# Attention backward on one core: the key-side score gradients are taken from DMA transposes, and the sums for dk, dv and dq are kept in SBUF

## The chip, the core and the metric

The kernel runs on one NeuronCore of a Trainium2 chip. TensorE (PE) multiplies matrices from SBUF into PSUM, VectorE (DVE) and ScalarE (ACT) work element by element and empty PSUM, GpSimd (POOL) does some element work from SBUF, and SyncE (SP) issues the transfers. Each engine takes its instructions in order and waits on semaphores for the others. The metric is the device time of one execution in microseconds.

## What is computed

The program returns the output of a gated mix of multi-head attention and a state-space convolution, and the gradients of twelve of its inputs, for a sequence of 2048 tokens and a width of 576. The change touches the attention alone: 32 heads of width 18.

```python
def _A_ref(x, wqkv, wo):
    B, S, D = x.shape
    H = 32
    Dh = D // H
    qkv = (lambda x, *d: x.transpose(*d))((x @ wqkv).reshape(B, S, 3, H, Dh), 2, 0, 3, 1, 4)
    q, k, v = qkv[0], qkv[1], qkv[2]
    scores = jnp.einsum("bhqd,bhkd->bhqk", q, k) * (Dh ** -0.5)
    p = _softmax(scores, axis=-1)
    o = jnp.einsum("bhqk,bhkd->bhqd", p, v)
    return (lambda x, *d: x.transpose(*d))(o, 0, 2, 1, 3).reshape(B, S, D) @ wo
...
_out, _vjp = jax.vjp(_f, A_x, A_wqkv, A_wo, B_A_re, B_A_im, B_B_re, B_B_im, B_C_re, B_C_im, B_log_dt, B_Dskip, gate_w)
_grads = _vjp(grad_out)
```

With P the softmax and dP = dO V^T, the backward pass needs dS = P (dP - delta), where delta is the sum of dO times O over a head; then dq = dS K (summed over keys), dk = dS^T Q and dv = P^T dO (both summed over queries).

## The kernel before

Four stages follow each other: the projections, which leave q, k, v and dO in DRAM in two layouts; attention, forward and backward; the products with the output projection, which read the attention output O; and the state-space part.

Attention works on eight groups of four heads (NG = 8, j = 0 to 3 within a group). Each head fills a strip of 32 partitions, and heads on different strips can share a pass of PE. The 2048 tokens are cut into four blocks of 512 (NQ = 4, KB = 512) and sixteen tiles of 128 (NT = 16, index i). There are four kinds of score tile, each 128x512, and 2048 of each kind over the program:

- P1: keys on partitions, queries along the row. `qk` multiplies K and Q, ACT takes the exponential and leaves the tile PT. It feeds the forward sum over keys, accA.
- P2: the same layout. `qk` multiplies V with dOaT (dO over the softmax sum, with -delta in an extra column), DVE multiplies by PT and leaves ds. It feeds the sum for dq, accB.
- P3S: queries on partitions, keys along the row. The score is computed again, and ACT takes the exponential again (eb). It feeds the sum for dv, accA.
- P3D: the same layout. dP is computed again and DVE multiplies by eb. It feeds the sum for dk, accB.

Every score tile has one matmul of 19 rows by 128 columns over 512 columns (written as `19*128 19x512`), one instruction of ACT or DVE, and one accumulating matmul (`pv`), whose output is 32 partitions by 512. The sums run in PSUM over all sixteen tiles; the last tile of a block calls `finish`, which copies the sum out. At the end of a P1 block, `post_forward` turns the sum to token layout (ps_o), divides by the softmax sum (O_tok, in SBUF), forms dOa and delta on POOL and DVE, and turns dOa back (dOaT). `post_grad` turns dq, dk and dv of a whole group and stores them in dqkv_d.

The order is written by hand. The list `blocks` pairs a P1 block with a P2 block, or a P3S block with a P3D block. A step issues two score matmuls for ACT and two for DVE, on the other pair of heads, then the accumulating matmuls of two steps before (LAG = 2), then ACT's and DVE's instructions. `run_piece` issues one piece of `post_forward` or `post_grad` in every third step. PE, ACT, DVE and POOL run in this order; SP's transfers are placed by the scheduler. PSUM gives three slots each to tags S (P1, P3S and all the transposes) and dP (P2, P3D), one to accA and one to accB. All tiles of a group that are loaded (`load_group`) have two buffers.

The state-space part has 36 DMA transposes of its own (L930), of E1e tiles of 128x4096 in 2-byte elements.

Of the kernel before, what the change touches and what calls it, by code (L numbers as in the profile page):

```python
# [20 lines left out]
def build(tc, aps, dbg_aps=None, stages=("s1", "attn", "post", "s4", "final")):  # L21
# [39 lines left out]
    with ExitStack() as gctx:  # L61
# [15 lines left out]
        mid1_cm = tc.tile_pool(name="mid1", bufs=1)  # L77
        mid1 = mid1_cm.__enter__()
        O_tok = mid1.tile([P, NT, D], BF, name="O_tok")
# [6 lines left out]
        Vtok_d = dram.tile([P, NT * H * HP], BF, name="Vtok_d")  # L86
        dO_d = dram.tile([P, NT, D], BF, name="dO_d")
# [168 lines left out]
        if "attn" in stages:  # L256
# [4 lines left out]
            with ExitStack() as ctx:  # L261
                ctx.enter_context(tc.manual_schedule(engines={mybir.EngineType.PE, mybir.EngineType.Activation, mybir.EngineType.DVE, mybir.EngineType.Pool}))
                ga = ctx.enter_context(tc.tile_pool(name="ga", bufs=2))
                ptp = ctx.enter_context(tc.tile_pool(name="ptp", bufs=18))
                work = ctx.enter_context(tc.tile_pool(name="awork", bufs=2))
                apsp = ctx.enter_context(tc.tile_pool(name="aps", bufs=1, space=bass.MemoryType.PSUM))
                ident_f = const.tile([P, P], F32, name="ident_f")
# [5 lines left out]
                grp_t = {}  # L273
                dOa2 = []
                for u in range(2):
                    dOa_u = work.tile([P, NT, 4, HP], BF, tag=f"dOa{u}", bufs=1, name=f"dOa{u}")
                    nc.gpsimd.memset(dOa_u, 0.0)
                    dOa2.append(dOa_u)

                def load_group(g):  # L280
                    T = {}
                    for nm, src in (("QaT", QaT_d[g]), ("KaT", KaT_d[g]), ("VaT", VaT_d[g])):
                        T[nm] = ga.tile([P, S], BF, tag=nm, name=nm + "_g")
                        nc.sync.dma_start(T[nm], src)
                    for nm, src in (("Qtok", Qtok_v), ("Ktok", Ktok_v), ("Vtok", Vtok_v)):
                        T[nm] = ga.tile([P, NT, 4, HP], BF, tag=nm, name=nm + "_g")
                        nc.sync.dma_start(T[nm], src[:, :, 4 * g:4 * g + 4, :])
                    T["dO"] = ga.tile([P, NT, 4, DH], BF, tag="dO", name="dO_g")
                    nc.sync.dma_start(T["dO"].rearrange("p t a b -> p t (a b)"), dO_d[:, :, 4 * g * DH:4 * (g + 1) * DH])
                    T["dOa"] = dOa2[g % 2]  # L290
                    T["dOaT"] = ga.tile([P, S], BF, tag="dOaT", name="dOaT_g")
                    for nm in ("dqT", "dkT", "dvT"):
                        T[nm] = ga.tile([P, S], BF, tag=nm, bufs=1, name=nm + "_g")
                    T["PT"] = {}
                    grp_t[g] = T

                def ps1(tag, name, dt=F32, w=KB):
                    return apsp.tile([P, w], dt, tag=tag, bufs=3, name=name)

                later = []  # L300

                def pieces(fs):
                    later.append(list(fs))

                def run_piece():
                    if later:
                        later[0].pop(0)()
                        if not later[0]:
                            later.pop(0)

                def post_forward(g, b, acc):
                    T = grp_t[g]
                    t0 = b * TPQ
                    c0 = g * 4 * DH
                    h0 = 4 * g
# [6 lines left out]
                    def f1():  # L322
                        st["po"] = apsp.tile([P, TPQ, 4, HP], F32, tag="S", bufs=3, name="ps_o")
                        for qi in range(TPQ):
                            nc.tensor.transpose(st["po"][:, qi, :, :].rearrange("p a b -> p (a b)"), st["oT"][:, qi * P:(qi + 1) * P], ident_f)
                        rl = work.tile([P, TPQ, 4], F32, tag="rl", name="rl")
                        nc.vector.reciprocal(rl, st["po"][:, :, :, DH])  # L327
                        rlb = rl.unsqueeze(3).to_broadcast([P, TPQ, 4, DH])
                        Ov = O_tok[:, t0:t0 + TPQ, c0:c0 + 4 * DH].rearrange("p t (a b) -> p t a b", b=DH)
                        dOv = T["dO"][:, t0:t0 + TPQ, :, :]  # L330
                        da = T["dOa"][:, t0:t0 + TPQ, :, :]
                        nc.vector.tensor_tensor(Ov, st["po"][:, :, :, 0:DH], rlb, op=A.mult)
                        nc.gpsimd.tensor_tensor(da[:, :, :, 0:DH], dOv, rlb, op=A.mult)  # L333
                        prod = work.tile([P, TPQ, 4, DH], F32, tag="prod", name="prod")
                        nc.gpsimd.tensor_tensor(prod, da[:, :, :, 0:DH], Ov, op=A.mult)
                        dl = work.tile([P, TPQ, 4], F32, tag="dl", name="dl")
                        nc.vector.tensor_reduce(dl, prod, axis=AX.X, op=A.add)
                        nc.gpsimd.tensor_scalar(da[:, :, :, DH], dl, -1.0, None, op0=A.mult)

                    def f2():  # L340
                        pt = apsp.tile([P, KB], BF, tag="S", bufs=3, name="ps_doT")
                        for qi in range(TPQ):
                            nc.tensor.transpose(pt[:, qi * P:(qi + 1) * P],
                                                T["dOa"][:, t0 + qi, :, :].rearrange("p a b -> p (a b)"), ident_bf)
                        nc.scalar.copy(T["dOaT"][:, b * KB:(b + 1) * KB], pt)

                    return [f0, f1, lambda: None, f2]

                def post_grad(g, nm, which):
                    T = grp_t[g]  # L350
                    c0 = which * D + g * 4 * DH
                    HT = NT // 2

                    def half(u):
                        def f():
                            pt = apsp.tile([P, HT, 4, HP], BF, tag="S", bufs=3, name="ps_dt")
                            for t in range(HT):
                                tt_ = u * HT + t
                                nc.tensor.transpose(pt[:, t, :, :].rearrange("p a b -> p (a b)"), T[nm][:, tt_ * P:(tt_ + 1) * P], ident_bf)
                            dtk = work.tile([P, HT, 4, DH], BF, tag="dtk", name="dtk")  # L360
                            nc.scalar.copy(dtk, pt[:, :, :, 0:DH])
                            nc.sync.dma_start(dqkv_d[:, u * HT:(u + 1) * HT, c0:c0 + 4 * DH], dtk.rearrange("p t a b -> p t (a b)"))
                        return f
                    return [half(0), half(1)]

                def qk(kind, g, b, i, j):
                    T = grp_t[g]
                    r0 = HP * j
                    if kind == "P1":
                        l, r = T["KaT"], T["QaT"]  # L370
                    elif kind == "P2":
                        l, r = T["VaT"], T["dOaT"]
                    elif kind == "P3S":
                        l, r = T["QaT"], T["KaT"]
                    else:
                        l, r = T["dOaT"], T["VaT"]
                    tg = "S" if kind in ("P1", "P3S") else "dP"
                    ps = ps1(tg, "ps_" + kind)
                    mm(ps, lhsT=l[r0:r0 + DA, i * P:(i + 1) * P], rhs=r[r0:r0 + DA, b * KB:(b + 1) * KB], tile_position=(r0, 0))
                    return ps  # L380

                e3 = {}

                def elem(kind, g, b, i, j, ps):
# [70 lines left out]
                for n in range(len(act_s) + LAG):  # L455
                    cur = []
                    if n < len(act_s):
                        for (blk_, i, jj) in (act_s[n], dve_s[n]):
                            if blk_ is None:
                                continue  # L460
# [765 lines left out]
```

## Time and profile before

| | |
|---|---|
| time, median of 3 runs | 5774.57 us (5774.31 to 5775.28) |
| profiled execution | 5779.55 us, span 5777.8 us |
| PE busy over the span | 3879.6 us, 67%, 34473 matmuls |
| DVE busy over the span | 4022.2 us, 70% |
| ACT busy over the span | 3207.5 us, 56% |
| POOL busy over the span | 607.7 us, 11% |
| DVE, ACT, PE busy from 1200 to 1600 us | 362.45, 321.77, 382.92 of 400 us |
| DMA share there | 0.05 |

A row of the costliest groups reads: line, engine, operation, output<-inputs, shapes and count; then busy time, mean time of one in ns, and the idle time of the engine just before such instructions, with what ended it. In a timeline a row gives the start, the length and, at its end, how many instructions ran back to back. The engine called SPq in it is SP's queue, and its rows are issues of transfers. A matmul's end is modelled, and matmuls on different strips overlap, so the distance from one start to the next says more of PE than its busy time.

### The profile page before, as it was taken

The page shows a single profiled execution, that of the slowest core. Times are in us where ns is not written, and L with a number is a line of the kernel's source. Part 1 is how long each engine was busy: PE and PEld are TensorE (multiplying, and loading weights), DVE is VectorE, ACT ScalarE, POOL GpSimd, SP SyncE. Part 2 cuts the span into 40 slices and gives each one's busy share as a digit, 9 for nine tenths or more (in the row PEclk, how much of TensorE's full clock was granted, in tenths as well). Part 3 has the DMA queues.
Part 4 walks back from the last instruction along what each step waited for, and adds up shares of the span by engine and source line. Part 5 has one row for each costly group of instructions (what it writes and reads, how often), then busy time and mean ns, then how long its engine had stood idle before and what let it go on. Part 6 is the DMA issues. An engine that isn't in the chain of part 4 may idle for free. (4 is left out here: it accounts for less than half of the span.)

```text
span 5777.8 us, 90570 instructions
## 1 busy us (share of the span) xinstructions
PE 3879.6 (67%) x34473; PEld 1452.2 (25%) x34473; DVE 4022.2 (70%) x7458; ACT 3207.5 (56%) x6150; POOL 607.7 (11%) x845
## 2 busy tenths in 40 slices
PE   6687999999999999999999987832222222222221
PEld 4462111212212122121221237711111222222210
DVE  4334899898998989989899973330017667776668
ACT  3336788787887778878788562310004444444421
POOL 1000000000000000000000000030002333333330
PEclk9999999999999999999999558855555555555555
DMA  2122000101001010010000013032235444444436
GB/s 96 59 74 65 11 2 7 25 1 29 3 7 25 1 29 3 7 25 1 20 3 1 7 38 118 32 102 65 66 92 124 113 113 113 115 115 115 111 92 168
DMA packets 599927, 316.83 MB, mean 55 GB/s; under 512 B 523198, under 2 KB 571520, under 8 KB 589634
## 3 DMA queue, kind: packets, MB, share of 16 engines
q1 hardware_dynamic: 599490, 311.05, 20.8%
q8 instruction: 269, 4.41, 0.3%
q14 instruction: 168, 1.38, 0.1%
HBM read 203.53 MB, written 69.71 MB: 47 GB/s over the span
## 5 line engine op out<-in xcount | busy, mean ns | idle before, releaser
L398 DVE TENSOR_TENSOR ds<-ps_P3D,eb 128x512 bf16<-128x512 f32 x2048 | 1293.5, 686 | 128.0 <-PE ps_P3D L30 83.9
L398 DVE TENSOR_TENSOR ds<-ps_P,PT 128x512 bf16<-128x512 f32 x2048 | 1288.8, 686 | 100.6 <-PE ps_P L30 96.7
L394 ACT ACTIVATE eb<-ps_P3S 128x512 bf16<-128x512 f32 x2048 | 1109.0, 595 | 258.8 <-PE ps_P3D L30 181.7
L390 ACT ACTIVATE PT<-ps_P 128x512 bf16<-128x512 f32 x2048 | 1107.5, 596 | 213.0 <-PE ps_P L30 131.7
L30 PE MATMUL ps_P3D<-VaT_g,dOaT_g 19*128 19x512 bf16 x2048 | 791.4, 593 | 16.6 <-DVE ds L398 16.0
L30 PE MATMUL ps_P<-dOaT_g,VaT_g 19*128 19x512 bf16 x2048 | 757.1, 591 | 0.5 <-DVE ds L398 0.4
L30 PE MATMUL ps_P<-QaT_g,KaT_g 19*128 19x512 bf16 x2048 | 675.1, 597 | 72.1 <-DMA KaT_g<-KaT_d 37.8
L30 PE MATMUL ps_P3S<-KaT_g,QaT_g 19*128 19x512 bf16 x2048 | 671.2, 597 | 30.9 <-ACT eb L394 28.4
L30 PE MATMUL accA<-PT,Vtok_g 128*32 128x512 bf16 x2048 | 625.4, 608 | 6.6 <-DMA Vtok_g<-Vtok_d 6.5
L30 PE MATMUL accA<-eb,dOa 128*32 128x512 bf16 x2048 | 626.3, 608 | 0.0
L30 PE MATMUL accB<-ds,Qtok_g 128*32 128x512 bf16 x2048 | 625.8, 608 | 0.0
L30 PE MATMUL accB<-ds,Ktok_g 128*32 128x512 bf16 x2048 | 625.0, 607 | 0.0
L30 PE MATMUL uvr<-RX,E1e 128*128 128x64 bf16 x576 | 72.4, 291 | 647.9 <-DVE E1e L891 647.9
L30 PEld LDWEIGHTS <-E1e 128*128 128x128 bf16 x1152 | 119.8, 124 | 724.3 <-DVE E1e L891 629.4
L333 POOL TENSOR_TENSOR dOa<-dO_g,rl 128x288 bf16<-128x288 bf16 x32 | 21.5, 673 | 2663.7 <-DVE rl L327 2663.7
L824 DVE TENSOR_SCALAR xs<-xs,msk 128x3072 bf16<-128x3072 bf16 x21 | 21.4, 1020 | 375.9 <-DMA xs<-in_A_x_dram 375.9
L30 PEld LDWEIGHTS <-dOa 128*32 128x32 bf16 x2048 | 107.4, 101 | 634.6 <-issue 634.6
L837 ACT COPY mst<-psM 128x512 f32<-128x512 f32 x36 | 22.1, 613 | 438.4 <-PE psM L30 362.2
L30 PEld LDWEIGHTS <-Vtok_g 128*32 128x32 bf16 x2048 | 106.6, 101 | 585.1 <-issue 577.7
L30 PE MATMUL psM<-xs,gyp 128*32 128x128 bf16 x576 | 54.7, 550 | 259.8 <-DMA xs<-in_A_x_dram 133.6
L30 PEld LDWEIGHTS <-KaT_g 19*128 19x128 bf16 x2048 | 104.9, 99 | 480.6 <-issue 452.0
L30 PE MATMUL ybp<-Rw,E1n 128*128 128x31 bf16 x1152 | 71.4, 233 | 224.9 <-POOL Rw L972 219.5
(332 smaller groups left out, 5561.0 us busy)
## 6 DMA issues: line engine op xcount, KB each, us to landing
abuf<-ath_d SPq DMA_DIRECT2D x36, 1024.0 KB
thb<-ath_d SPq DMA_DIRECT2D x36, 1024.0 KB
T0w<-Kp_d SPq DMA_DIRECT2D x36, 512.0 KB
dqkv_d<-dtk SPq DMA_DIRECT2D x48, 144.0 KB
dqkv_tok<-dqkv_d SPq DMA_DIRECT2D x1, 6912.0 KB
Md_d<-mst SPq DMA_DIRECT2D x144, 36.0 KB
x_tok<-in_A_x_dram SPq DMA_DIRECT2D x2, 2304.0 KB
ga_d<-ga_st SPq DMA_DIRECT2D x16, 288.0 KB
```

Source lines behind the costliest of these rows:

```text
L30: return nc.tensor.matmul(out, lhsT=lhsT, rhs=rhs, start=start, stop=stop, **kw)
L333: nc.gpsimd.tensor_tensor(da[:, :, :, 0:DH], dOv, rlb, op=A.mult)
L390: nc.scalar.activation(out, ps, ACT.Exp)
L394: nc.scalar.activation(out, ps, ACT.Exp)
L398: nc.vector.tensor_tensor(out, ps, e, op=A.mult)
L824: nc.vector.tensor_scalar(xs[:, dl, :, :], xs[:, dl, :, :], msk[:, dl:dl + 1], None, op0=A.mult)
L837: nc.scalar.copy(mst[:, :, 0:P], psM)
```

## The change

P3D goes. P1, P2 and P3 (the former P3S) are issued together in one loop over G, a step of which has two of each. A "unit" is a group and a query block (32 units of 32 steps). P2 and P3 of a unit run OFF = 37 steps behind its P1.

- When the four heads of a key tile i have their ds, SP issues one DMA transpose of the 128x2048 tile. It leaves dsT, queries on partitions, which feeds the sum for dk. There are four buffers of ds and three of dsT (two key tiles each).
- The sums for dv, dq and dk no longer run in PSUM over sixteen tiles. Bursts of eight matmuls (`dv_burst`, `dq_burst`), or two halves of eight narrower ones (`dk_half`), fill one PSUM slot (accB), and DVE adds it to a sum in SBUF in f32. Sums of dv and dk run on over the four query blocks of a group.
- `post_forward` has its POOL instructions on DVE now, and stores O to DRAM (O_d) per unit; the stage after attention loads it as O_tok. `store_grad` turns f32 sums of 512 tokens, with one copy of 128x288 on ACT each.
- PSUM: four slots S, two dP, one accO, one accB. VaT, Ktok and Qtok of a group have one buffer, QaT, KaT and Vtok two.

```diff
-        O_tok = mid1.tile([P, NT, D], BF, name="O_tok")
+        O_d = dram.tile([P, NT, D], BF, name="O_d")
...
+                    for nm, src, nb in (("QaT", QaT_d[g], 2), ("KaT", KaT_d[g], 2), ("VaT", VaT_d[g], 1)):
+                        T[nm] = ga.tile([P, S], BF, tag=nm, bufs=nb, name=nm + "_g")
...
-                        nc.gpsimd.tensor_tensor(da[:, :, :, 0:DH], dOv, rlb, op=A.mult)
-                        nc.gpsimd.tensor_tensor(prod, da[:, :, :, 0:DH], Ov, op=A.mult)
+                        nc.vector.tensor_tensor(da[:, :, :, 0:DH], U["dO"], rlb, op=A.mult)
+                        nc.vector.tensor_tensor(prod, da[:, :, :, 0:DH], Ob, op=A.mult)
...
+                def dv_burst(g, b, kq, half):
+                    acc = accB("accV")
+                    for n_ in range(2):
+                        ii = 2 * half + n_
+                        for j in range(4):
+                            mm(acc[HP * j:HP * (j + 1), :], lhsT=U["dOa"][:, ii, j, :], rhs=U["eb"].pop((kq, ii, j)),
+                               start=(n_ == 0), stop=(n_ == 1), tile_position=(0, HP * j))
+                    def ev():
...
+                            nc.vector.tensor_tensor(a_, a_, acc, op=A.add)
...
+                def dk_half(g, b, p, h, st):
+                    for qb in (2 * h, 2 * h + 1):
+                        for j in range(4):
+                            mm(acc[HP * j:HP * (j + 1), 0:2 * P].rearrange("p (a b) -> p a b", b=P), lhsT=grp_t[g]["Qtok"][:, b * TPQ + qb, j, :],
+                               rhs=U["dsT", p][:, :, j * TPQ + qb, :], start=(qb == 0), stop=(qb == 3), tile_position=(0, HP * j))
...
+                        if s == 4 and b == NQ - 2 and g + 1 < NG:
+                            load_group(g + 1)
...
+                            par_ = (s2 + OFF) % 2
+                            jo = 2 * (1 - par_) + x
+                            rows.append(("P3", g, b, (kq, ii), jo, row("P3", g, b, T["QaT"][:, qt * P:(qt + 1) * P], T["KaT"][:, kq * KB:(kq + 1) * KB], jo)))
+                            j2 = 2 * par_ + (1 - x)
+                            rows.append(("P2", g, b, i2, j2, row("P2", g, b, T["VaT"][:, i2 * P:(i2 + 1) * P], U["dOaT"], j2)))
+                    if G % 4 == 1 and G2 >= 4:
+                            evs.append(dv_burst(g, b, q_ // 2, q_ % 2))
+                    if G % 4 == 2 and G2 >= 5:
+                            evs.append(dq_burst(g, b, q_))
+                    if G % 4 in (3, 0) and G2 >= 10:
+                            e_ = dk_half(g, b, q_, h_, dkst)
...
+                            if U["dsn", i] == 4:
+                                nc.sync.dma_start_transpose(out=U["dsT", p][:, i % 2, :, :], in_=U["ds"][i].rearrange("p j q -> p (j q)"))
...
+                nc.sync.dma_start(O_tok, O_d)
```

The order of the built programs shows it at three places. The first is PE in the middle of attention. Before, a step of a P3S and a P3D block is four score matmuls and the accumulating matmuls of an earlier step (numbers tell buffers apart; each matmul has its weight load ahead of it):

```order
L30 LDWEIGHTS QaT_g_7148
L30 MATMUL ps_P3S_11556<-KaT_g_7150,QaT_g_7148 128x512
L30 LDWEIGHTS QaT_g_7148
L30 MATMUL ps_P3S_11558<-KaT_g_7150,QaT_g_7148 128x512
L30 LDWEIGHTS dOaT_g_7162
L30 MATMUL ps_P3D_11560<-VaT_g_7152,dOaT_g_7162 128x512
L30 LDWEIGHTS dOaT_g_7162
L30 MATMUL ps_P3D_11562<-VaT_g_7152,dOaT_g_7162 128x512
L30 LDWEIGHTS dOa0_7144
L30 MATMUL accA_11241<-eb_11528,dOa0_7144 32x512
```

Now, on PE, a step has six score matmuls, and then a burst; this one is the first half of a dk burst, from dsT:

```order
L30 MATMUL ps_P1_11242<-QaT_g_8512,KaT_g_8514 128x512
L30 LDWEIGHTS QaT_g_7147
L30 MATMUL ps_P3_11244<-KaT_g_7149,QaT_g_7147 128x512
L30 LDWEIGHTS VaT_g_7151
L30 MATMUL ps_P2_11246<-dOaT_10725,VaT_g_7151 128x512
L30 LDWEIGHTS KaT_g_8514
L30 MATMUL ps_P1_11248<-QaT_g_8512,KaT_g_8514 128x512
L30 LDWEIGHTS QaT_g_7147
L30 MATMUL ps_P3_11250<-KaT_g_7149,QaT_g_7147 128x512
L30 LDWEIGHTS VaT_g_7151
L30 MATMUL ps_P2_11252<-dOaT_10725,VaT_g_7151 128x512
L30 LDWEIGHTS Qtok_g_7157
```

P3D and its weights dOaT are gone, P1 stands beside P2 and P3 of a later place in the loop (here of another group, as the buffer numbers of QaT and KaT show), and the accumulating matmuls come as bursts.

The second place is DVE in the middle of a unit, now:

```order
L519 TENSOR_TENSOR ds_28045<-ps_P2_28025,PT_26776 128x512
L519 TENSOR_TENSOR ds_28045<-ps_P2_28031,PT_26776 128x512
L379 TENSOR_TENSOR dvacc_25831<-dvacc_25831,accV_28033 128x512
L519 TENSOR_TENSOR ds_28045<-ps_P2_28056,PT_26776 128x512
L519 TENSOR_TENSOR ds_28045<-ps_P2_28062,PT_26776 128x512
L396 TENSOR_TENSOR dqa_27817<-dqa_27817,accQ_28064 128x512
L519 TENSOR_TENSOR ds_28113<-ps_P2_28089,PT_26839 128x512
L519 TENSOR_TENSOR ds_28113<-ps_P2_28095,PT_26839 128x512
L519 TENSOR_TENSOR ds_28113<-ps_P2_28123,PT_26839 128x512
L519 TENSOR_TENSOR ds_28113<-ps_P2_28129,PT_26839 128x512
L420 TENSOR_TENSOR dkacc_25799<-dkacc_25799,accK_28097 128x256
```

In four steps DVE has eight products and three additions; before, it had sixteen products in the same work (eight P2, eight P3D) and no addition.

The third place is SP where one group gives way to the next (the first rows are stores and loads of the old group, VaT is the next group's and QaT that of the group after it):

```order
L525 DMA_TRANSPOSE dsT_11662<-ds_11693 128x16x128 [waits DMAHW6_49,DVE_49]
L323 DMA O_d_79<-Ob_11784 128x4x72 [waits DMAHW7_49,DVE_49]
L294 DMA dO_b_12837<-dO_d_80 128x4x72 [waits DMAHW0_49,DVE_49]
L525 DMA_TRANSPOSE dsT_11823<-ds_11770 128x16x128 [waits DMAHW1_49,DVE_49]
L282 DMA QaT_g_13000<-QaT_d_73 128x2048 [waits DMAHW2_49,PE_49]
L282 DMA VaT_g_8516<-VaT_d_75 128x2048 [waits DMAHW3_49,PE_49]
L525 DMA_TRANSPOSE dsT_11823<-ds_11855 128x16x128 [waits DMAHW4_49,DVE_49]
L282 DMA KaT_g_13002<-KaT_d_74 128x2048 [waits DMAHW5_49]
L341 DMA dqkv_d_81<-dtk_11939 128x4x72 [waits DMAHW6_49,Activation_49]
L285 DMA Ktok_g_8520<-Ktok_d_77 128x16x128 [waits DMAHW7_49,PE_49]
```

The transposes are a new kind of row between the loads, and VaT and Ktok wait for PE here; before, the next group's VaT had a buffer of its own and stood far ahead of its use. The DMAHW marks are eight completion counters that are used in turn, so a transfer waits for ones eight or so places back.

More of the change, by code (lines that the diff above doesn't have):

```diff
@@ L345, in f2 @@
[L345 to L350, printed above, removed]
-                    c0 = which * D + g * 4 * DH
[L352 to L364, printed above, removed]
@@ L367, in qk, with row @@
+                def row(kind, g, b, l, r, j):
                     T = grp_t[g]
                     r0 = HP * j
[L369 to L377, printed above, removed]
@@ L427, in build @@
[L427 to L430 removed]
+                    tg, nb = ("dP", 2) if kind == "P2" else ("S", 4)
+                    ps = apsp.tile([P, KB], F32, tag=tg, bufs=nb, name="ps_" + kind)
+                    mm(ps, lhsT=l[r0:r0 + DA], rhs=r[r0:r0 + DA], tile_position=(r0, 0))
+                    return ps
+                NST = 2 * NT
+                NU = NG * NQ
```

319 lines of the change are left out of this document (174 added, 145 removed).

## The prediction

> **What bounds the kernel now.** First the page: the span, against 5779.55 us for the profiled execution (5774.57 is the median of the runs shown), and its costliest groups.
>
> ```profile
> span 5777.8 us, 90570 instructions
> L398 DVE TENSOR_TENSOR ds<-ps_P3D,eb 128x512 bf16<-128x512 f32 x2048 | 1293.5, 686 | 128.0 <-PE ps_P3D L30 83.9
> L398 DVE TENSOR_TENSOR ds<-ps_P,PT 128x512 bf16<-128x512 f32 x2048 | 1288.8, 686 | 100.6 <-PE ps_P L30 96.7
> L394 ACT ACTIVATE eb<-ps_P3S 128x512 bf16<-128x512 f32 x2048 | 1109.0, 595 | 258.8 <-PE ps_P3D L30 181.7
> L390 ACT ACTIVATE PT<-ps_P 128x512 bf16<-128x512 f32 x2048 | 1107.5, 596 | 213.0 <-PE ps_P L30 131.7
> ```
>
> Instructions of one engine overlap at their ends, so the pitch is busy time by count: 1293.5/2048 = 0.632 us for a DVE product, 1109.0/2048 = 0.541 us for an exp on ACT. The timeline shows where the stage begins and ends, and a piece from its middle.
>
> ```profile
> 463.75 0.61 PE L30 MATMUL ps_P<-QaT_g,KaT_g 19*128 19x512 bf16 x3 [12.21 <-DMA KaT_g<-KaT_d]
> ...
> 1299.41 7.00 DVE L398 TENSOR_TENSOR ds<-ps_P,PT 128x512 bf16<-128x512 f32 x11
> ...
> 1300.62 2.32 ACT L390 ACTIVATE PT<-ps_P 128x512 bf16<-128x512 f32 x4 [0.20 <-PE ps_P L30]
> ...
> 1301.95 0.61 PE L30 MATMUL accA<-PT,Vtok_g 128*32 128x512 bf16 x2
> ...
> 1302.50 0.61 PE L30 MATMUL ps_P<-QaT_g,KaT_g 19*128 19x512 bf16 x2
> ...
> 1303.18 0.61 PE L30 MATMUL accA<-PT,Vtok_g 128*32 128x512 bf16 x2
> ...
> 3412.74 1.06 PE L359 MATMUL ps_dt<-ident_bf,dkT_g 128*128 128x128 bf16 x8
> ```
>
> Attention takes 3413.80 - 463.75 = 2950 us, half of the kernel. DVE runs eleven products without a gap in 7.00 us; a step of two takes 1.25 us, the same as PE from one accA to the next (1301.95 to 1303.18). ACT rests 0.20 in 2.5. So DVE ends last; ACT is next at 2 x 0.541 = 1.08 a step.
>
> PE is the third. At the end of the stage nothing holds it, and its own pace shows:
>
> ```profile
> 3408.59 1.03 PE L30 MATMUL accB<-ds,Qtok_g 128*32 128x512 bf16 x4
> ...
> 3408.99 0.64 PE L30 MATMUL accA<-eb,dOa 128*32 128x512 bf16 x2
> ...
> 3409.55 1.03 PE L359 MATMUL ps_dt<-ident_bf,dvT_g 128*128 128x128 bf16 x8
> ```
>
> Four accumulating matmuls on different 32-column strips run together; a second round on the same strips starts 0.40 later, and a matmul of another kind 0.56 after that. Above, the kinds change every 0.55. I use 0.43 for a round and 0.11 for a change of kind.
>
> The clock needs a look, because the rows disagree.
>
> ```profile
> 800.00:1200.00 400.00, 383.20 (x2356) 81.58 (x2356) 362.95 (x582) 320.75 (x595) 7.00 (x13) 1.00 0.05 12
> 3250.00:3300.00 50.00, 48.71 (x300) 9.19 (x296) 46.45 (x75) 40.70 (x76) 0.00 (x0) 0.50 0.00 1
> ```
>
> The last columns are granted clock, DMA share and GB/s. At 1.00 and at 0.50 the matmuls keep 0.61 us; shorter ones are found in a few microseconds only:
>
> ```profile
> 3199.25 0.39 PE L30 MATMUL accB<-ds,Ktok_g 128*32 128x512 bf16 x2
> ```
>
> So I take the slow pace for the whole stage. The Trainium skill, "TensorE: Matmul & The Clock Gate", section "Single matmul latency", gives (219 + 512)/1.2 = 609 ns for the gated clock and (398 + 512)/2.4 = 379 ns for the full one; by that rule PE stays gated under a granted 1.00, and the rows of 0.61 and 0.39 agree. By its full clock the sum would be the first rival's.
>
> **The change, part by part.** *Removed:* 2048 P3D score matmuls and 2048 products on DVE (1293.5 us of the bound). What is late next is ACT, which keeps all 4096 exps. A new step holds four exps, six score matmuls, two products and bursts of accumulating matmuls (the order rows of PE).
>
> *ACT:* 4 x 0.541 = 2.165 a step. *DVE:* 2 x 0.632 = 1.26, and in four steps one addition each for dv and dq (128x512) and one for dk (128x256). Price: 0.43 for the half size by the row below, 0.69 for the full size by the products' mean; (2 x 0.69 + 0.43)/4 = 0.45. Sum 1.71.
>
> ```profile
> 4373.75 0.43 DVE L949 TENSOR_TENSOR tz<-HG,par 128x256 f32<-128x256 f32 x1
> ```
>
> *PE:* the six score matmuls name row strips so that three run together: two rounds, 0.97 with the change of kind; the bursts are two rounds too (the dk ones are twice as many, half as wide), 0.97. Sum 1.94. In the tightest loop (0.05 for a hand-over: ps_doT's matmuls, below, end at 514.13, their copy starts at 514.16), the step's last exp frees the PSUM slot of the next step's last P3 matmul: 0.05 + 0.43 + 0.11 + 0.86 (burst) + 0.11 + 0.61 (the following step's first score matmul) + 0.05 = 2.22, then four exps 2.165: two steps in 4.39, 2.19 each. With nothing to spare, I look at how ACT and PE at like loads get on now, where only P1 runs (ACT 1.08, PE 1.08):
>
> ```profile
> 504.72 2.17 ACT L390 ACTIVATE PT<-ps_P 128x512 bf16<-128x512 f32 x4 [0.17 <-PE ps_P L30]
> ...
> 507.07 1.08 ACT L390 ACTIVATE PT<-ps_P 128x512 bf16<-128x512 f32 x2 [0.18 <-PE ps_P L30]
> ```
>
> 2.35 for two steps, 1.17 each, 8% over ACT's work. I take half of that, since four slots replace three: **2.25**; ends 2.165 and 2.34. P2 runs 37 steps behind P1, in 1024 steps of each: 37 x 1.17 = 43; 987 x 2.25 = 2221; 37 at DVE's 1.71 = 63; the last 16 about 6.
>
> *The pieces between.* Per query block, the forward result goes through oT, ps_o, dOa and ps_doT:
>
> ```profile
> 508.83 0.59 ACT L320 COPY oT<-accA 128x512 f32<-128x512 f32 x1 [0.67 <-PE accA L30]
> 509.47 1.12 PE L325 MATMUL ps_o<-ident_f,oT 128*128 128x128 f32 x4 [0.68 <-ACT oT L320]
> 510.68 0.26 DVE L327 RECIPROCAL rl<-ps_o 128x16 f32<-128x16 f32 x1 [59.09 <-PE ps_o L325]
> 510.97 0.46 DVE L332 TENSOR_TENSOR O_tok<-ps_o,rl 128x288 bf16<-128x288 f32 x1
> ...
> 511.83 0.69 POOL L335 TENSOR_TENSOR prod<-dOa,O_tok 128x288 f32<-128x288 bf16 x1
> 512.55 0.45 DVE L337 TENSOR_REDUCE dl<-prod 128x16 f32<-128x288 f32 x1 [1.13 <-POOL prod L335]
> ...
> 513.52 0.61 PE L343 MATMUL ps_doT<-ident_bf,dOa 128*128 128x128 bf16 x4 [2.93 <-POOL dOa L338]
> 514.16 0.59 ACT L345 COPY dOaT_g<-ps_doT 128x512 bf16<-128x512 bf16 x1 [4.75 <-PE ps_doT L343]
> ```
>
> POOL's three move to DVE, where 0.46 for 288 elements bounds each of the two products: DVE then holds about 2.3 in one run, in front of the products that free PE's two dP slots. Two copies cost ACT 1.08. PE's 1.12, DVE's run less its rest in two steps (2.3 - 2 x 0.54 = 1.2), less PE's rest of 0.3, delay the next exps by 2.0: 3.1 a block, x32 = 99. Each store of a gradient (32 dq, 64 dk and dv) puts four f32 transposes (1.12) and a copy of half a dtk ahead of a step's exps (the whole is 0.64, so about 0.36): less a little rest 1.4, x96 = 134.
>
> ```profile
> 1394.92 0.64 ACT L361 COPY dtk<-ps_dt 128x576 bf16<-128x576 bf16 x1 [0.63 <-ACT PT L390]
> ```
>
> Of these 233, ACT's own work is 69 (1.08 x 32 + 0.36 x 96), the low end; the excess of 164 doubled gives the high one, 397.
>
> *Group changes.* VaT has one buffer now: its load waits for the old group's last P2, and the first P2 of the new one follows within a step (the SP rows).
>
> ```profile
> 458.73 0.33 SPq L284 DMA_DIRECT2D QaT_g<-QaT_d  x1
> 459.11 0.43 SPq L284 DMA_DIRECT2D KaT_g<-KaT_d  x1
> ...
> 460.68 5.05 SPq L287 DMA_DIRECT2D Ktok_g<-Ktok_d  x1
> ...
> 465.78 1.99 SPq L287 DMA_DIRECT2D Vtok_g<-Vtok_d  x1
> ...
> 473.08 0.61 PE L30 MATMUL accA<-PT,Vtok_g 128*32 128x512 bf16 x2 [6.45 <-DMA Vtok_g<-Vtok_d]
> ```
>
> Two such loads landed 5.0 us after the first issue (458.73 to 463.75), a Vtok 7.3 after its own. The gap costs about 5; Ktok and Qtok, with 4 and 3 steps to land in, another 3: 8 x 7 = 56; ends 3 and 20 each. At the start Vtok comes two loads earlier, and ACT waits 5.
>
> *The DMA transposes.* 512 of 128x2048. The trace has 36 of 128x4096, issued from SP:
>
> ```profile
> L930 SPq DMA_TRANSPOSE E1n<-E1e x36: 4821/4908/6015, 4345.2 to 5566.9; - x36
> 4348.00:4349.00 1.00, 0.00 (x0) 0.00 (x0) 0.00 (x0) 0.00 (x0) 0.00 (x0) 0.50 1.18 217
> ```
>
> Half the size: 2.45 of SP, and 0.52 MB at 217 GB/s, 2.42 of the queues. One is due every two steps, 4.5 us, so I cost them at nothing; ACT's work is the cover. The change adds waits: a dk burst waits for its transpose six steps on, and DVE's first product of a key tile for the transpose of four tiles earlier, also six steps on; behind it stand the additions and the products that PE's dP slots need. Issue and data take 2.45 + 2.42 us, some two steps, so four are left, 9 us, even behind a load that holds SP 5.05. If the price went by instruction and not by size, 512 x 4.9 = 2509 plus 109 of lead-in and tail would still be no more than ACT's pace gives. The Trainium skill, "VectorE: DVE Perf Modes", section "The three transpose paths", has 1309 ns for one 128x128 block by DMA; by that rule 16 blocks would be 20.9 and the sum, an estimate, 10.7 ms for the stage. The 32 blocks of these rows take 4.9 us of SP, 0.15 each: the trace does not agree.
>
> *After the stage.* O_tok is read back, 2.3 MB, like go_tok now:
>
> ```profile
> 3419.87 0.59 SPq L519 DMA_DIRECT2D go_tok<-in_grad_out_dram  x1
> 3429.00:3431.00 2.00, 1.31 (x10) 0.78 (x10) 0.76 (x4) 0.82 (x4) 0.00 (x0) 0.50 0.34 112
> ```
>
> About 10 us; PE's next transposes stand 4.5 after the stage now, so 8 is added.
>
> **Sum.** 43 + 2221 + 63 + 6 + 99 + 134 + 56 + 5 = 2627, plus 8; 2635 against 2950 is -315. 5779.55 - 315 = 5465; the median is 5 lower: **5460**.
>
> **Rivals.**
> - *PE at full clock, or pieces that hide:* the step falls to 2.165 (-84), the pieces to 69 (-164): 5212; the middle is 5336. For it: the short spell of 0.39. Against: the same mix keeps 0.61 now. 18%.
> - *More stalls:* step 2.34 (+89), pieces 397 (+164), 20 a group change (+84): 5797 with all, 5630 in the middle. For it: one buffer for each accumulator and in-order PE. 14%.
> - *Slower:* the queues transpose more slowly beside loads and three busy engines than alone. Then ds's four buffers fill, DVE waits, and PE and ACT behind it. At p us each the stage is 512p + 46 (lead-in) + 63; it reaches 2942 at p = 5.5, and no gain is left. At the longest SP time seen, 6.0, it is 3181, +239 with the 8 after it: 6014. Against: 2.45 is far off. 12%. The skill's figure above would end far beyond this; the trace speaks against it.
> - *The change doesn't do what it says:* transposes kept apart by waits for earlier transfers, hiding nothing more than is saved: within 0.2%. Each names only transfers several places back (SP rows). 4%.
>
> Forecast 52%. Range 5280 to 5700: all of the forecast, most of the first two rivals. Faster by over 0.2% (about what a measurement can tell from none) 0.84, same 0.04, slower 0.12.
>
> **What would show it.** ACT in runs of four exps with a pitch near 2.25; DMA_TRANSPOSE near 2.45 on SP; DVE never waiting for a DMA at a ds; seven gaps of 5 to 10 us before VaT matmuls. DVE idle before ds by DMA would prove the slower rival, matmuls of 0.39 the first one, and a step over 2.4 with PE named as releaser the second.

## The result, and the profile after

The changed kernel takes 5259.16 us (median of 4 runs, 5253.75 to 5261.09) against 5774.92 for the kernel before on the same chip: ratio 0.910, 95% interval 0.909 to 0.912. It is 516 us faster. The forecast was 315 faster, and the time lies 21 us below the range. The direction held, and so did the loop of waits that was forecast for the step; the prices put into it did not.

The page of the changed kernel, its span and its costliest groups (the columns are those of the page before):

```profile
span 5257.9 us, 87333 instructions
L519 DVE TENSOR_TENSOR ds<-ps_P,PT 128x512 bf16<-128x512 f32 x2048 | 1328.6, 686 | 470.1 <-PE ps_P L30 262.0
L510 ACT ACTIVATE PT<-ps_P 128x512 bf16<-128x512 f32 x2048 | 1226.5, 603 | 154.5 <-PE ps_P L30 102.6
L514 ACT ACTIVATE eb<-ps_P 128x512 bf16<-128x512 f32 x2048 | 1236.0, 605 | 19.8 <-PE ps_P L30 19.3
```

The 2048 products with eb are gone, and DVE now waits (470 us before its products, mostly for PE). The stage, from the timeline:

```profile
459.85 0.61 PE L30 MATMUL ps_P<-QaT_g,KaT_g 19*128 19x512 bf16 x4 [12.32 <-DMA KaT_g<-KaT_d]
...
501.94 0.60 PE L30 MATMUL ps_P<-KaT_g,QaT_g 19*128 19x512 bf16 x1
...
2806.34 0.60 PE L30 MATMUL ps_P<-KaT_g,QaT_g 19*128 19x512 bf16 x1
...
2886.69 0.44 PE L338 MATMUL ps_dt<-ident_f,dkacc 128*128 128x128 f32 x2 [0.17 <-DVE dkacc L420]
2896.16 0.37 PE L554 MATMUL pt_o<-ident_bf,O_tok 128*128 128x128 bf16 x2 [9.03 <-DMA O_tok<-O_d]
```

Attention takes 2887.1 - 459.9 = 2427 us instead of 2950, and 200 less than the forecast's 2627. Behind it, PE waits 9.0 for O_tok; everything after the stage takes 7 us longer than before, where 8 were forecast. So the whole error lies in the stage. It has 42 us of lead-in (before 501.9), 2304 for the 987 full steps, and 81 for the tail. The rows of one loop through PE and ACT, which takes two steps (others between them are left out):

```profile
1300.72 0.62 ACT L514 ACTIVATE eb<-ps_P 128x512 bf16<-128x512 f32 x1
...
1301.38 0.58 PE L30 MATMUL ps_P<-KaT_g,QaT_g 19*128 19x512 bf16 x1
...
1301.92 1.04 PE L30 MATMUL accQ<-ds,Ktok_g 128*32 128x512 bf16 x8
...
1302.80 0.62 ACT L514 ACTIVATE eb<-ps_P 128x512 bf16<-128x512 f32 x1
1302.90 0.60 PE L30 MATMUL ps_P<-QaT_g,KaT_g 19*128 19x512 bf16 x1
...
1303.54 0.60 ACT L510 ACTIVATE PT<-ps_P 128x512 bf16<-128x512 f32 x1
1304.03 0.59 ACT L514 ACTIVATE eb<-ps_P 128x512 bf16<-128x512 f32 x1
1304.51 0.60 ACT L510 ACTIVATE PT<-ps_P 128x512 bf16<-128x512 f32 x1
1304.98 0.62 ACT L514 ACTIVATE eb<-ps_P 128x512 bf16<-128x512 f32 x1
...
1305.65 0.58 PE L30 MATMUL ps_P<-KaT_g,QaT_g 19*128 19x512 bf16 x1
```

Follow one slot (a PSUM tile of tag S). The last exp of a step (1300.72) ends at 1301.34, and the P3 matmul that needs its slot starts at 1301.38. The burst starts 0.54 later, the next step's score matmuls 0.98 after that (1302.90), and the first exp on them at 1303.54. Four exps follow at a pitch of 0.48, the last ends at 1305.60, and the P3 matmul two steps after the first starts at 1305.65. That is 4.27 us for two steps: the loop of the forecast, which had 4.39. Over 23 undisturbed steps (1258.05 to 1307.16) a step takes 2.135 us; the forecast took 2.25. ACT is not full: from the last exp of a step to the first of the next it takes 0.74 here (1302.80 to 1303.54) and not 0.48, since the first has to wait for its score matmul. Nor is PE: a P3 matmul waits in every step for the last exp of the step before, and the same work takes PE 1.94 a step where the exps are shorter (x6 below).

### The profile page after: what moved, and what is told of

Read it like the earlier page. It is cut to its first block, busy times and chain, and to the rows that moved or that the text cites. A ratio compares the mean times of both kernels' runs of the same rounds, so it can differ in the third digit from the quotient of the medians.

```text
span 5257.9 us, 87333 instructions
## 1 busy us (share of the span) xinstructions
PE 3442.0 (65%) x34473; PEld 1477.7 (28%) x34473; DVE 3203.6 (61%) x6274; ACT 3065.4 (58%) x6102; POOL 551.4 (10%) x750
## 5 line engine op out<-in xcount | busy, mean ns | idle before, releaser
L514 ACT ACTIVATE eb<-ps_P 128x512 bf16<-128x512 f32 x2048 | 1236.0, 605 | 19.8 <-PE ps_P L30 19.3
L30 PE MATMUL ps_P<-dOaT,VaT_g 19*128 19x512 bf16 x2048 | 1197.4, 601 | 29.6 <-DMA VaT_g<-VaT_d 28.5
L30 PE MATMUL ps_P<-KaT_g,QaT_g 19*128 19x512 bf16 x2048 | 1164.7, 593 | 7.6 <-ACT PT L510 7.6
L30 PE MATMUL ps_P<-QaT_g,KaT_g 19*128 19x512 bf16 x2048 | 1053.9, 615 | 14.8 <-DMA KaT_g<-KaT_d 12.3
L30 PE MATMUL accO<-PT,Vtok_g 128*32 128x512 bf16 x2048 | 331.1, 631 | 1.1 <-DMA Vtok_g<-Vtok_d 1.1
L30 PEld LDWEIGHTS <-VaT_g 19*128 19x128 bf16 x2048 | 197.4, 98 | 437.0 <-issue 404.8
L30 PE MATMUL accK<-dsT,Qtok_g 128*32 128x256 bf16 x4096 | 314.7, 406 | 1.8 <-DVE dqa L396 1.0
L30 PE MATMUL accQ<-ds,Ktok_g 128*32 128x512 bf16 x2048 | 266.9, 620 | 1.2 <-DVE dvacc L379 1.2
L30 PE MATMUL accV<-eb,dOa 128*32 128x512 bf16 x2048 | 266.9, 620 | 0.6 <-DVE dkacc L420 0.6
L30 PEld LDWEIGHTS <-QaT_g 19*128 19x128 bf16 x2048 | 178.8, 100 | 51.3 <-issue 27.6
```

The costliest lines, as they stand in the source:

```text
L30: return nc.tensor.matmul(out, lhsT=lhsT, rhs=rhs, start=start, stop=stop, **kw)
L514: nc.scalar.activation(e, ps, ACT.Exp)
```

## The experiments

All times are medians. The kernel before took 5774.9 to 5781.0 in the five sets of runs, so differences of a few us between sets say nothing.

### Are the DMA transposes hidden, and by how much?

```diff
-    nc.sync.dma_start_transpose(out=U["dsT", p][:, i % 2, :, :], in_=U["ds"][i].rearrange("p j q -> p (j q)"))
...
-    rhs=U["dsT", p][:, :, j * TPQ + qb, :]
+    rhs=U["dsp", p][:, :, j, qb * P:(qb + 1) * P]      # ds of two key tiles, in one tile
```

> The 512 DMA transposes are left out; the dk matmuls, of the same number and shape, read ds itself, so dk is not the gradient here, and everything else is as in the changed kernel (5259 us). If the transposes are hidden, as the forecast has it: 5259, within 15. If their traffic (DMA share 0.70 in the stage) holds up the group loads or the engines' own access to SBUF: lower, up to the 28 us that PE waits for VaT for the loads alone, and 50 or more if the step of 2.135 us itself falls.

Measured (x1): 5256.16 us, ratio 0.9094 (0.9081 to 0.9108): no difference from the changed kernel. The windows (busy time and count of PE, PE loads, DVE, ACT and POOL; granted clock, DMA share, GB/s), first of the changed kernel, then of this one:

```profile
1200.00:1600.00 400.00, 394.88 (x2864) 103.68 (x2862) 302.82 (x507) 366.93 (x716) 0.00 (x0) 0.50 0.70 126
```

```profile
1200.00:1600.00 400.00, 395.46 (x2864) 103.54 (x2859) 304.33 (x508) 367.40 (x717) 0.00 (x0) 0.50 0.06 13
```

The DMA share falls from 0.70 to 0.06, and the three engines do the same work in the same 400 us. The transposes cost nothing here. (The run also gives ds twice the buffers, so it shows what the transposes and a lack of ds buffers cost together.) The second run asks what room is left.

```diff
+    sc_ = work.tile([P, 4 * TPQ, P], BF, tag="dsX", bufs=1, name="dsX")
+    nc.sync.dma_start_transpose(out=sc_, in_=U["ds"][i].rearrange("p j q -> p (j q)"))
```

> Each ds is transposed twice, the second time into a tile that nothing reads. How near is the changed kernel to the slower rival, where the queues set the time? If a transpose takes 2.42 us of the queues, as half of the E1n rows gives, two steps need 4.84 and have 4.27: the stage becomes 512 x 4.84 + 109 = 2587 instead of 2427, in all about 5420. If the share of 0.70 is work that cannot be packed (0.70 x 4.66 us from one transpose to the next = 3.26 each), it is 512 x 6.52 + 109 = 3447, in all 6280. SP's own 2 x 1.87 would still fit.

Measured (x2): 5757.6 us, ratio 0.996 (0.994 to 0.998). The stage is about 2427 + 498 = 2925 us, so a transpose takes (2925 - 109)/1024 = 2.75 us: between the two prices, nearer to the 2.42 worked out from E1n. A window of this run, a row of its waits (waiting instruction, releaser: total us, times, longest), and a piece of SP's timeline:

```profile
1000.00:1400.00 400.00, 349.30 (x2366) 79.91 (x2364) 245.90 (x420) 306.21 (x594) 0.00 (x0) 0.50 1.13 199
```

```profile
DVE ds L519 <- DMA dsX<-ds: 466.2, 220, 5.8
```

```profile
1309.89 2.75 SPq L525 DMA_TRANSPOSE dsT<-ds  x1
1312.73 2.68 SPq L527 DMA_TRANSPOSE dsX<-ds  x1
1315.47 3.56 SPq L525 DMA_TRANSPOSE dsT<-ds  x1
```

In this piece SP issues almost without a pause; 199 GB/s move, and DVE waits for transposes before it writes ds: this is what the slower rival would look like. But from 1000 to 1400 us SP itself waits some 78 us for DVE ahead of transposes, so the 2.75 holds such pauses and is an upper bound for one. Whether SP, the queues behind it or these waits set it isn't told apart. Transposes would take over if those of two steps needed more than 4.27 us; the one that the changed kernel has in two steps, at 2.75, fills 64% of that.

### Which engine sets the step: ACT, PE, or the loop through both?

Three slots for ACT's tiles (tag S, which the transposes on PE share) in place of four:

```diff
-    tg, nb = ("dP", 2) if kind == "P2" else ("S", 4)
+    tg, nb = ("dP", 2) if kind == "P2" else ("S", 3)
```

> Three PSUM slots for the tiles that ACT reads instead of four. Loop theory: the last P3 matmul of a step then waits for the first exp of its own step: first score matmul + 0.65 + 0.62 + 0.04, then 0.54 to the burst and 0.97 to the next step's first: 2.82 instead of 2.135, 987 x 0.685 = 676 more, 5935, less what the pieces between (200 us) then hide. ACT alone, or PE alone, as the bound: 5259 within 20.

Measured (x11): 5879.83 us, ratio 1.018 (1.016 to 1.020): slower than before. Its timeline on PE:

```profile
1300.10 0.60 PE L30 MATMUL ps_P<-QaT_g,KaT_g 19*128 19x512 bf16 x1
...
1301.38 0.58 PE L30 MATMUL ps_P<-KaT_g,QaT_g 19*128 19x512 bf16 x1 [0.25 <-ACT PT L510]
...
1302.90 0.60 PE L30 MATMUL ps_P<-QaT_g,KaT_g 19*128 19x512 bf16 x1
...
1305.70 0.60 PE L30 MATMUL ps_P<-QaT_g,KaT_g 19*128 19x512 bf16 x1
```

The step is 2.80, where the loop gives 2.82, and the P3 matmul at 1301.38 waits for the first exp of its own step, as expected. Neither engine got more work: one PSUM slot less costs 621 us, more than the whole change gains.

Less work for ACT alone, and for PE alone:

```diff
-    nc.scalar.activation(e, ps, ACT.Exp)
+    nc.scalar.activation(e, ps[:, 0:KB // 2], ACT.Exp)
```

> The two P3 exps of each step compute 256 columns instead of 512, and the dv matmuls read those 256 twice: ACT's work falls by about 2 x 0.22 us in a step (0.41 for a copy of 288 columns against 0.61 for 512), PE's and DVE's stay. dv is not the gradient here. Loop theory: the two-step loop of 4.27 holds four exps, two of them now 0.22 shorter, 3.83, step 1.92, PE's own work, and 987 x 0.21 = 210 less, 5050. ACT alone as the bound: 4 x 0.534 - 0.44 = 1.70, below PE's 1.94, so the same 5050 or lower. PE alone as the bound: 5259 within 20.

```diff
-    for n_ in range(2):
+    for n_ in range(1):      # in dv_burst and dq_burst
```

> The dv and dq bursts issue only the first of their two rounds (four matmuls instead of eight), so half of dv and dq is left out; ACT's and DVE's work stays. Loop theory: each two-step loop holds one burst, one of two loops has it 0.43 shorter in four steps: 8.54 - 0.43 = 8.11 for four, 2.03 a step, 987 x 0.107 = 106 less, 5153. ACT alone as the bound: 5259 within 20. PE alone as the bound: twice that, 0.215 a step, 5047.

Measured: 5100.71 us with half the P3 exps (x6; 158 less than the changed kernel) and 5177.2 (x8) with the lighter bursts (82 less). Less work on either engine shortens the step. ACT alone as the bound would have left the second run at 5259, PE alone the first one. Both gains are about three quarters of what the loop gives (210 and 106). The steps themselves come nearer to it. In the first run the undisturbed step is 1.94, from one burst to the next, where 1.92 was worked out:

```profile
1281.68 1.04 PE L30 MATMUL accQ<-ds,Ktok_g 128*32 128x512 bf16 x8
...
1283.62 0.62 PE L30 MATMUL accK<-dsT,Qtok_g 128*32 128x256 bf16 x8
```

In the second run four steps take 8.19 (1261.49 to 1269.68), where 8.11 was worked out. By these steps 192 and 86 us would be gained; in the first run the other 34 are lost where pieces stand between the steps, and how is not shown. In the second run ACT has a queue of ready tiles, and its own pace can be read:

```profile
1299.66 0.60 ACT L510 ACTIVATE PT<-ps_P 128x512 bf16<-128x512 f32 x1
1300.15 0.59 ACT L514 ACTIVATE eb<-ps_P 128x512 bf16<-128x512 f32 x1
...
1304.47 0.69 ACT L510 ACTIVATE PT<-ps_P 128x512 bf16<-128x512 f32 x1
1304.94 0.70 ACT L514 ACTIVATE eb<-ps_P 128x512 bf16<-128x512 f32 x1
```

Eleven pitches from 1299.66 to 1304.94 are 5.28 us: 0.480 for an exp, 1.92 for the four of a step, while each is shown as 0.59 to 0.70 long. The forecast had 0.541 and 2.165. The Trainium skill, "ScalarE: Activation LUTs", section "What ACT_TABLE_LOAD costs", has 186 ns + 0.833 ns per column for an instruction with immediate scale and bias, and an overlap of about 93 ns from one to the next; an estimate by that page is 0.52 for 512 columns. The measured 0.48 is lower still.

### Can another order open the loop?

The bursts move between the two rounds of score matmuls of a step; the second run moves DVE's additions with them.

```diff
+    rows_x(0)                # score matmuls of the first pair of heads
     # bursts
+    rows_x(1)
     for (kind, g, b, i, j, ps) in rows:      # ACT's and DVE's instructions
...
     for e_ in evs:           # additions: behind both products
         e_()
```

> The bursts stand between the two rounds of score matmuls of a step instead of behind both; nothing else is changed. Theory: the step of 2.135 us is a loop through both engines (last exp frees a PSUM slot, last P3 matmul, burst, first score matmul of the next step, four exps at 0.48, 0.48, 0.48 and 0.64: 4.27 for two steps), and neither engine is full. With the burst between, the slot has come free long before, and the step falls to the fuller engine's own work, PE 0.97 + 0.97 = 1.94 or ACT 4 x 0.48 = 1.92: about 1.95, 987 x 0.185 = 180 us less, about 5080. Rival: ACT is full at 0.534 an exp (the pitch of 0.48 is only a catching up): no change, 5259 within 20. Second rival: the dv burst, which takes the exps of the step before, now waits for them: 5300 or more.

Measured (x3): 5771.35 us, ratio 0.999 (0.998 to 1.000). The whole gain is gone. PE's waits in this run name the cause:

```profile
PE accK L30 <- DVE dqa L396: 205.1, 215, 1.0
PE accQ L30 <- DVE dvacc L379: 172.0, 170, 1.0
PE accV L30 <- DVE dkacc L420: 74.3, 159, 0.7
...
PE accK L30 <- DVE dqa L394: 31.5, 31, 1.0
...
PE accQ L30 <- DVE dvacc L376: 25.1, 24, 1.1
PE accV L30 <- DVE dkacc L418: 23.6, 56, 0.7
```

Together 532 us, against 512 lost. All bursts share one PSUM slot, accB (the expectation calls it a bank). A burst that comes earlier in the step finds the slot still full, because the addition that empties it stands behind two products on DVE. The expectation's second rival had the direction, but named a wait for exps as the cause. The next run shows that it is accB.

```diff
+    h_n = len(rows) // 2
+    for n_, (kind, g, b, i, j, ps) in enumerate(rows):
+        if n_ == h_n:
+            for e_ in evs:
+                e_()
```

> As x3 (burst between the two rounds of score matmuls), and the addition of the burst's result moves too: it stands between the two products of the step on DVE and no longer behind both, so that the one PSUM bank of the bursts comes free before the next burst. If x3 lost its 512 us by that bank alone, they are all back. If the loop over the score slots is then what is left out (theory), PE sets the step: 0.54 + 0.97 + 0.54, since the kind of matmul now changes one time more, 2.05 against 2.135: 987 x 0.085 = 84 us less than the changed kernel, 5175; with 1.94 it would be 5065. If ACT is full at 0.534 an exp: 5259 within 20. If the bank still holds PE, because the addition waits behind a product: over 5300.

Measured (x9): 5283.45 us, ratio 0.914 (0.913 to 0.916). The waits for accB are gone and with them 488 us, so that cause is shown. But the order gains nothing: 24 us slower than the changed kernel, where 84 less was expected. Its timeline, with the first score matmul of three second rounds, and one exp and the matmul that waits for it:

```profile
1300.50 0.60 PE L30 MATMUL ps_P<-QaT_g,KaT_g 19*128 19x512 bf16 x1
...
1302.46 0.60 PE L30 MATMUL ps_P<-QaT_g,KaT_g 19*128 19x512 bf16 x1
...
1302.59 0.62 ACT L520 ACTIVATE eb<-ps_P 128x512 bf16<-128x512 f32 x1
...
1303.26 0.58 PE L30 MATMUL ps_P<-KaT_g,QaT_g 19*128 19x512 bf16 x1
...
1304.77 0.60 PE L30 MATMUL ps_P<-QaT_g,KaT_g 19*128 19x512 bf16 x1
```

Steps of 1.96 and 2.31 take turns. In the long one, a P3 matmul starts 0.05 after the exp that frees its slot (1302.59 + 0.62 = 1303.21), with the burst behind it; in the short one ACT then waits for PE. So the wait for a slot has moved to another place in the step. ACT needs 1.92 and PE 1.94, four slots lie between them, and 2.135 comes out in either order, so the 24 us are not in these steps; 7 of them are longer waits for VaT (35 us in place of 28). More slots were not tried: this kernel, like the one before, lays out eight of 128x512 in f32 (4 S, 2 dP, accO, accB), and none is spare.

### The pieces between the steps

```diff
-    ("VaT", VaT_d[g], 1)
+    ("VaT", VaT_d[g], 2)
```

> VaT gets two buffers like QaT and KaT, so its load no longer waits for the last P2 of the old group. If the seven waits of 28.5 us in all are paid in full: 5259 - 28 = 5231. If Ktok or Qtok, with one buffer each, end the wait next: a gain of 0 to 15 only.

Measured (x4): 5230.33 us, ratio 0.9049 (0.9036 to 0.9063), 29 less. The changed kernel had lost just that, in seven waits of 4.1 on average:

```profile
PE ps_P L30 <- DMA VaT_g<-VaT_d: 28.5, 7, 5.1
```

Ktok and Qtok, with one buffer each, hold PE up neither in the changed kernel nor here.

The stores of gradients: `store_grad` keeps its transfer only, from a constant tile.

```diff
-    nc.tensor.transpose(pt[:, t, :, :].rearrange("p a b -> p (a b)"), src[:, t * P:(t + 1) * P], ident_f)
-    nc.scalar.activation(dtk, pt[:, :, :, 0:DH], ACT.Copy, scale=scale)
...
+    nc.sync.dma_start(dqkv_d[:, t0:t0 + TPQ, c0:c0 + 4 * DH], dtk0.rearrange("p t a b -> p t (a b)"))
```

> The 96 stores of gradients send a constant tile: their 384 f32 transposes on PE and 96 copies on ACT are left out, and dq, dk and dv of the attention are constants here. By the trace of the changed kernel a store costs its step 1.05 (3.13 instead of 2.08): 5259 - 101 = 5158. By the forecast's 1.4: 5125. By ACT's own 0.36 alone (the rest hidden): 5224.

Measured (x5): 5175.16 us, ratio 0.895 (0.894 to 0.897), 84 less: 0.88 a store. In the changed kernel's timeline, the step with a store takes 3.13 (1340.68 to 1343.81) and the next one 2.08:

```profile
1340.68 0.60 PE L30 MATMUL ps_P<-QaT_g,KaT_g 19*128 19x512 bf16 x1
...
1342.76 1.11 PE L338 MATMUL ps_dt<-ident_f,dvacc 128*128 128x128 f32 x4
...
1343.81 0.60 PE L30 MATMUL ps_P<-QaT_g,KaT_g 19*128 19x512 bf16 x1
1343.91 0.41 ACT L340 ACTIVATE dtk<-ps_dt 128x288 bf16<-128x288 f32 x1 [0.53 <-PE ps_dt L338]
...
1345.89 0.60 PE L30 MATMUL ps_P<-QaT_g,KaT_g 19*128 19x512 bf16 x1
```

PE's transposes are paid, 1.05 in this step; ACT's copy is not, since ACT has run dry by then (0.53 idle) and is done with it before the next score tile is there. This split is read from the timeline: the run takes both away at once.

### Is it the removed products or the new order?

```diff
+    rows.append(("P3D", g, b, (kq, ii), jd, row("P3D", g, b, U["dOaT"][:, ii * P:(ii + 1) * P], T["VaT"][:, kq * KB:(kq + 1) * KB], jd)))
...
+    nc.vector.tensor_tensor(d_, ps, U["eb"][(i[0], i[1], j)], op=A.mult)
...
-    rhs=U["dsT", p][:, :, j * TPQ + qb, :]
+    rhs=U["d3"].pop((kq, ii, j))
```

> The loop, the sums in SBUF and the order of the changed kernel, but dk from recomputed tiles as before: two more score matmuls and two more products in each step, no DMA transposes, and the dk addition as wide as dv's. Theory: the gain comes from the products taken off DVE; with four at 0.63 and three additions of 0.69 in four steps DVE needs 3.05 a step, above everything else: 987 x (3.05 - 2.135) = 903 more than the changed kernel, 6160, so slower than the kernel before, which has no additions on DVE. Rival: the gain comes from the new order, with P1, P2 and P3 in one loop: below 5600.

Measured (x7): 8092.04 us, far above the 6160 expected. The sign spoke for the theory, the size didn't. A row of its waits:

```profile
DVE d L518 <- ACT eb L514: 1285.9, 991, 1.3
```

DVE waited for exps of its own step, and PE behind it. So the next run takes that wait away: P3D's rows come two steps later, `eb` and VaT get more buffers.

> As x7 (dk from recomputed tiles in the new loop), but each recomputed tile comes two steps after the exp that it is multiplied by, so that DVE does not wait for the last exp of the step, as it did in x7 (1286 us); VaT has two buffers. Theory, the products on DVE are what the change saves: at least DVE's own 3.05 a step, 6160 less x4's 29, about 6130; if two PSUM slots for four tiles keep PE's burst behind DVE (second slot free 0.65 + 0.63 + 0.63 after the first matmul, then 0.54 and 0.97): 3.46 a step, 6540. If x7's 8092 came from the two slots and not from the wait for the exp: over 7000. Rival, the order alone brings the gain: below 5600.

Measured (x12): 6699.54 us, ratio 1.160 (1.156 to 1.163), 1393 less than the run before it. The timeline on PE:

```profile
1301.57 0.60 PE L30 MATMUL ps_P<-QaT_g,KaT_g 19*128 19x512 bf16 x1
...
1303.03 0.58 PE L30 MATMUL ps_P<-dOaT,VaT_g 19*128 19x512 bf16 x1 [0.42 <-DVE ds L533]
...
1305.12 0.60 PE L30 MATMUL ps_P<-QaT_g,KaT_g 19*128 19x512 bf16 x1
```

The step is 3.55, near the 3.46 worked out for two dP slots that four tiles share. The new order by itself is therefore no gain: with recomputed tiles it is 921 us slower than the kernel before. That this is all due to DVE's work is not shown: here the four tiles' two PSUM slots set the step, DVE is busy 329 of 400 us (1200 to 1600), and its own work was put at 3.05. Removed products with the old order, and transposes there, were not tried, so how much of the 516 us each part of the change brings stays open.

### Both kernels beaten

VaT has two buffers; POOL rounds and scales the sum, a DMA transpose turns it, POOL packs it (and oT has one buffer in place of two):

```diff
-    nc.tensor.transpose(pt[:, t, :, :].rearrange("p a b -> p (a b)"), src[:, t * P:(t + 1) * P], ident_f)
-    nc.scalar.activation(dtk, pt[:, :, :, 0:DH], ACT.Copy, scale=scale)
+    nc.gpsimd.tensor_scalar(gb, src, scale, None, op0=A.mult)
+    nc.sync.dma_start_transpose(out=gT.rearrange("p t a b -> p t (a b)"), in_=gb)
+    nc.gpsimd.tensor_copy(dtk, gT[:, :, :, 0:DH])
```

> Two buffers for VaT (as x4, 5230), and the gradients are stored without PE and ACT: POOL, which does nothing in the stage, rounds the sum to bf16 and scales it, a DMA transpose of 128x512 turns it, POOL packs it for the store. If PE's and ACT's share of a store is what it costs, all of x5's 84 us come: 5146. If the transposes of the sums hold SP, so that those of ds or the loads come late, or POOL holds up the release of the sums that DVE writes: 5200 or more.

Measured (x10): 5163.41 us, ratio 0.8935 (0.892 to 0.895): 96 less than the changed kernel, and 17 short of the 5146 expected; so 67 of the 84 us of the stores came. A row of its waits is new; neither the changed kernel nor the run with two buffers for VaT has it:

```profile
PE accK L30 <- DMA Qtok_g<-Qtok_d: 29.9, 7, 5.8
```

With the other pieces gone, Qtok's one buffer now holds PE up at the seven group changes, which is more than the 17 us. That it is the whole reason is not shown.

## Why the prediction was right in kind and too small

| term | forecast, us | measured, us | from |
|---|---|---|---|
| lead-in | 43 | 42 | timeline |
| 987 steps | 2221 (2.25 each) | 2107 (2.135 each) | timeline, 23 steps |
| gradient stores | 134 | 84 | x5 |
| group changes | 56 | 29 | x4 |
| results of a block (post_forward) | 99 | 84 | what is left of 2304 |
| tail and end | 69 | 81 | timeline |
| wait at the start | 5 | within the lead-in | timeline |
| sum | 2627 | 2427 | |

**What bounds the kernel.** That DVE bound the kernel before rests on its trace, where DVE runs products without a gap and PE follows at its pace; no run took the products out of the old order. The runs show this much: in the new loop, with the products kept, the kernel is slower than before (x12), though PSUM slots have a share in that. That PE stays slow through the stage was right too: its score matmuls are 0.60 us long at a granted 0.50, as they were at 1.00.

**The step, the largest error (114 of 200 us).** The step that failed is the price of an exp: "the pitch is busy time by count", 1109.0/2048 = 0.541. That holds only if the engine never waits within a run. An exp is shown 0.60 long and its pitch is 0.48, so ACT can start one up to 0.12 late without any idle time being seen. In the kernel before, ACT waited for PE between the exps, and the idle time just ahead of them (259 and 213 us) was not all of it. The rows quoted for the lead-in showed it: four exps in 2.17 us, each 0.60 long, are 0.52 apart, but two in 1.08 are 0.48 apart. With 0.48, 0.48, 0.48 and 0.62 in place of 2.165, the forecast's own loop gives 2.22 + 2.06 = 4.28 for two steps, 2.14 a step; 2.135 was measured. That is some 55 of the 114 us. The other half is the allowance of 0.06 a step for stalls (59 us), taken from how ACT and PE met before. There were none. Because ACT's 2.165 served as a floor, both ends of the step (2.165 and 2.34) lay above the truth; only with the pieces at their low end as well (5212) did a rival reach below the measured time, and the range stopped short of that. Named as the bound, ACT was half right: it is one side of a loop, which x11, x6 and x8 show.

**The pieces (86 us).** For a store the forecast added PE's transposes and part of ACT's copy; the copy falls into ACT's rest, and 0.88 remains of 1.4. For a group change it had 5 for VaT and 3 for Ktok and Qtok; VaT took 4.1, the others nothing. The results of a block are near the forecast, as a remainder, not by a run of their own; as the 84 of the stores holds the few stores of the tail too, the remainder is rough.

**The transposes.** Costed at nothing, and x1 shows it to within the scatter of the runs. SP's price was below the 2.45 forecast, 1.87 in the median (its row: duration ns, least, median, most; then first and last start):

```profile
L525 SPq DMA_TRANSPOSE dsT<-ds x512: 1315/1871/4891, 506.1 to 2877.8; - x171
```

DVE waits for no transpose at a ds, as forecast. The slower rival falls: 2.75 us a transpose at most with twice as many of them (x2), where 5.5 were needed. The rival of more stalls falls with the step. The measured time lies in the reach of the first rival (5212 to 5460). It had two conditions: PE at full clock, which did not come, and pieces that hide, of which a part did; its step of 2.165 was closer than the forecast's, for another reason. The additions on DVE took 0.69 and 0.41, near their prices of 0.69 and 0.43.

## What to carry to other kernels

Before an average of busy time becomes a floor, look for two instructions in a row that waited for nothing: their distance is the engine's pace, and it can lie well under both the mean length and busy time by count. Where two engines of like load pass tiles through a few PSUM slots, write the loop through the slots out; with the right pitch it priced the step to 1%, and it said what one slot less would cost (2.82, measured 2.80), which neither engine's own sum says. It has limits: for another order of the bursts it promised 84 us, and 24 were lost (x9). And when an instruction moves ahead on one engine, the one that frees its buffer has to move on the other engine too: that was worth 488 us here.

## What the hardware showed beside that

- Exps of 128x512 from PSUM are 0.59 to 0.70 us long in the profile, yet follow each other at 0.480 us.
- DMA transposes of 128x2048 in 2-byte elements, SBUF to SBUF from SP, took at most 2.75 us each (199 GB/s over all transfers) where twice as many held up the stage (x2); beside three busy engines, at 126 GB/s, they cost these engines nothing measurable.
- The granted clock read 1.00 in the middle of the old stage (800 to 1200 us) and reads 0.50 in that of the new one, with the same score matmuls of 0.60 us: here the figure tells nothing of the pace, and the length of a matmul does.
